# Sketch attention with a gated FFN on one core: S1 and S2 on SyncE's queue, k on ScalarE's, and one weight-narrowing step placed inside the division

## The chip, the cores and the metric

The kernel runs on one core of a Trainium2 chip. The metric is the device time of one execution in microseconds (us), over several runs. A profile of one execution gives the time line: PE is TensorE's matrix multiplication, PEld its weight load, DVE is VectorE, ACT is ScalarE, POOL is GpSimd, SP is SyncE, which here does nothing but issue transfers.

## The reference

There are 4 batches (B) of 4 heads (H), 1088 positions (S) and 32 features (D). Attention uses a polynomial feature map phi with r = 8, so 64 features. Its output, seen as 4352 tokens of 128 features, goes through a gated FFN of width 1536.

```python
def phi(x):
    a = np.einsum('rd,bhsd->bhsr', S1, x)
    b = np.einsum('rd,bhsd->bhsr', S2, x)
    return np.einsum('bhsi,bhsj->bhsij', a, b).reshape(*x.shape[:-1], r * r)
q_p, k_p = (phi(q), phi(k))
kv = np.einsum('bhsf,bhsd->bhfd', k_p, v)
z = np.sum(k_p, axis=2)
num = np.einsum('bhsf,bhfd->bhsd', q_p, kv)
den = np.einsum('bhsf,bhf->bhs', q_p, z)[..., None] + 1e-06
attn = num / den
...
gate = 1.0 / (1.0 + np.exp(-(x @ w_gate)))
out = gate * (x @ w_val) @ w_out
```

S1, S2 and the three weight matrices arrive as 8-byte floating-point numbers, because of a division by a NumPy scalar; q, k and v are 4-byte.

## The kernel before

**The FFN sets the length.** The 4352 tokens are cut into chunks of 512, and the FFN's width into 12 blocks of 128. For one chunk and one block, `w1` multiplies the tokens `xT` with the gate and the value weights into one PSUM tile, `wave` (L314), ACT takes the sigmoid `sg` (L322), `glu` multiplies value and gate to `g` on DVE (L334), and `w2` accumulates g times the output weights in `moeout` (L271). `slot(group, waves)` is the hand-written order: it issues `group` first, then as many rounds of "glu of the wave before, w2 of two waves before, next w1" as `waves` says. All engines but SP run in the order in which the code is written; nothing is reordered.

**Weights are narrowed on the chip.** `load_w(n)` loads two blocks (n from 0 to 5) as pairs of 32-bit words into `w_in`. `narrow` makes 4-byte numbers of them. It is a generator with four steps, so that its instructions can be spread over the code: step 0 is a clamp of the high word on POOL (`cap`, L97) and a scaled copy of the low word on ACT (`tail`, L101). Step 1 is two bit operations on DVE (`head`, L105 and L109), step 2 a square on ACT (L117) and an integer addition on POOL (L118). Step 3 is one DVE instruction that writes `w_sb` (L121). `narrow_w(j, step)` does this for block j from 1 to 11. During the first chunk each `w1` of block j0 issues step 3 of block j0 + 1, step 0 of block j0 + 4, and steps 1 and 2 of block j0 + 2 (L323 to L329). So the wave of block 11 cannot start before step 3 of block 11, which is written down in the `w1` of block 10. S1 and S2 take the same four steps at the very start (`sr_in` to `sr`), with their clamp on DVE.

**Attention of batch 0 comes first,** before any FFN work. S1 and S2 are loaded replicated over the partitions (`load_s`, L129); each is 32 KB in rows of 256 bytes. k of batch 0 is loaded in two parts of 18 and 16 rows per partition, and q in two of 16 and 18 (L224 to L229). The order in the queues is: on SP k's second part, S1, q's first part, v, then weights; on ACT k's first part, S2. DVE then narrows S, transposes k's first part (`turn_k`, L378), makes the sketch matrices `st` and `sk`, transposes k's second part and q's first part (`turn_q`, L389). `kps` on PE (L401) follows, then the outer products `kp`, and `kv0` on PE. Before that PE runs three warm-up multiplications on ones (L243), six instructions in the trace.

**The division.** `dn(b, n)` issues the matmuls for denominators (`dps`, L620) and numerators (`nps`, L631) of one half of batch b: 512 tokens for n = 0, 576 for n = 1. It returns `divide`, which on DVE transposes the denominators, adds, takes the reciprocal (L641 to L644), spreads it with a transpose to `rb` (L648) and multiplies into `xT` (L657). `part(b, n)` issues a pending glu, then dn and its division. For batch 0 the second half is issued at L756 as the group of a slot with two waves; these are the waves of blocks 10 and 11 of the first chunk, and the first chunk needs only tokens of the first half.

Of the kernel before, what the change touches and what calls it, by code (L numbers as in the profile page):

```python
# [20 lines left out]
def kernel(  # L21
# [12 lines left out]
    nc = tc.nc  # L34
# [6 lines left out]
    NJ = DFF // P  # L41
    assert DM == H * D == P and D == 32 and R == 8 and S % 32 == 0

    T = S // 32

    NJK = 9
    KBASE = [0, 9, 17, 25]
# [78 lines left out]

    sr = const.tile([P, 2, D], F32, tag="sr", name="sr")
    sr_in = const.tile([P, 2, D, 2], I32, tag="sr_in", name="sr_in") if wide else None
    def load_s():  # L129
        for n, s_ in enumerate((S1, S2)):  # L130
            rows = bass.AP(tensor=s_.tensor, offset=s_.offset, ap=[[0, P // R], [D, R], [1, D]])
            if wide:
                (nc.sync, nc.scalar)[n].dma_start(
                    out=sr_in[:, n].rearrange("p d w -> p (d w)"), in_=rows.bitcast(I32)
                )
            else:
                (nc.sync, nc.scalar)[n].dma_start(out=sr[:, n], in_=rows)


    w_sb = const.tile([P, 3, NJ, P], F32, tag="w_sb", name="w_sb")  # L140
# [25 lines left out]
    def narrow_w(j, step):  # L166
        if not 0 <= j < NJ:
            return
        n, jj = divmod(j, 2)
        if wide:  # L170
            if step == 0:
                narrowing[j] = narrow(w_sb[:, :, j, :], w_in[n][:, :, jj], nc.gpsimd, j < NJ - 2)
            next(narrowing[j])


    def narrow_0(part, step):
        if wide:
            i = (slice(0, 2), slice(2, 3))[part]
            if step == 0:
                narrowing["0", part] = narrow(w_sb[:, i, 0], w_in[0][:, i, 0], nc.gpsimd)  # L180
            next(narrowing["0", part])


    def load_rows(src, b, t, parts=((0, T, nc.sync),)):
        for t0, t1, eng in parts:
            eng.dma_start(
                out=t[:, t0:t1, :],
                in_=bass.AP(
                    tensor=src.tensor,
                    offset=src[b, 0].offset + t0 * D,  # L190
                    ap=[[T * D, P], [1, (t1 - t0) * D]],
                ),
            )
# [15 lines left out]
    k_t, q_t, v_t = {}, {}, {}  # L209


    def new_kq(b):
        t = ld.tile([P, 2 * H * W1], F32, tag="kq", name="kq")
        kq = t[:, : 2 * T * D].rearrange("p (a t d) -> p a t d", a=2, t=T)
        k_t[b], q_t[b] = kq[:, 0], kq[:, 1]
# [5 lines left out]
            load_rows(q, b, q_t[b])  # L221

    new_kq(0)
    load_rows(k, 0, k_t[0], ((0, KBASE[2] + 1, nc.scalar), (KBASE[2] + 1, T, nc.sync)))  # L224
    load_s()
    load_rows(q, 0, q_t[0], ((0, T0, nc.sync),))
    v_t[0] = load_v(0)
# [74 lines left out]
    def w1():  # L302

        ci = moe["ci"]
        t0, tw = tok_chk[ci]
        jn = TCH // tw
        j0 = moe["w"] * jn
        wv = psm.tile([P, 2, TCH], F32, tag="wave", name="wave")

        tp = tw // 2 if ci == 0 and j0 == 0 else tw  # L310
        for o in range(0, tw, tp):
            for which in range(2):
                for jj in range(jn):
                    nc.tensor.matmul(  # L314
                        out=wv[:, which, jj * tw + o : jj * tw + o + tp],
                        lhsT=w_sb[:, which, j0 + jj, :],
                        rhs=xT[:, t0 + o : t0 + o + tp],
                        start=True,
                        stop=True,
                    )  # L320
        sg = sbG.tile([P, TCH], F32, tag="sg", name="sg", bufs=3)
        nc.scalar.activation(out=sg, in_=wv[:, 0], func=ACTF.Sigmoid)  # L322
        if ci == 0:  # L323
            narrow_w(j0 + 1, 3)
            if j0 == 0:
                narrow_0(1, 3)
            narrow_w(j0 + 4, 0)
            narrow_w(j0 + 2, 1)
            narrow_w(j0 + 2, 2)  # L329


        def glu():
            g = sbG.tile([P, TCH], F32, tag="g", name="g")
            nc.vector.tensor_tensor(out=g, in0=wv[:, 1], in1=sg, op=MUL)  # L334
            moe["todo"].append((ci, j0, jn, g.rearrange("p (j t) -> p j t", j=jn)))

        moe["gate"] = glu
        moe["w"] += 1
        if j0 + jn == NJ:
            moe["ci"] += 1  # L340
            moe["w"] = 0

    def glu():
        if moe["gate"] is not None:
            moe["gate"]()
            moe["gate"] = None

    def slot(group, waves):

        if group is not None:  # L350
            group()
        todo = moe["todo"]
        for _ in range(waves):
            more = moe["ci"] < len(tok_chk)
            if more and sum(tok_chk[moe["ci"]]) > moe["ready"]:
                break
            glu()


            last = moe["ci"] == len(tok_chk) - 1 and moe["w"] > 1  # L360
            lag = 3 if last else 2
            while len(todo) >= lag:
                w2(*todo.pop(0))
            if more:
                w1()
            elif not todo:
                break
            else:
                w2(*todo.pop(0))
# [59 lines left out]
    def half(t, n):  # L429
        return t.rearrange("p (n h w) -> p n h w", n=2, h=H)[:, n, :, : 32 * q_chk[n][1]]  # L430
# [184 lines left out]
    def dn(b, n):  # L615
        t0, tn = q_chk[n]
        w = 32 * tn
        dps = pso.tile([P, TCH], F32, tag=f"acc{(moe['sum'] + 1) % 2}", name="dps")
        for h in range(H):
            nc.tensor.matmul(  # L620
                out=dps[32 * h : 32 * h + 32, :w],
                lhsT=zb[b % 2][:, h, :],
                rhs=half(QP[b], n)[:, 2 * (h % 2) + h // 2, :],
                start=True,
                stop=True,
            )
        t = ps2.tile([P, 2, 512], F32, tag="two", name="nps")
        for h in range(H):
            for c in range(2):
                rows = slice(64 * c, 64 * c + 64)  # L630
                nc.tensor.matmul(  # L631
                    out=t[32 * h : 32 * h + 32, c, :w],
                    lhsT=ND[b][rows, 32 * h : 32 * h + 32],
                    rhs=half(QP[b], n)[rows, 2 * (h % 2) + h // 2, :],
                    start=True,
                    stop=True,
                )

        def divide(*parts):
            dT = sbA.tile([P, 9, 32], F32, tag="dT", name="dT")  # L640
            nc.vector.transpose(out=dT[:, :tn].rearrange("p t c -> p (t c)"), in_=dps[:, :w])  # L641
            rc = sbA.tile([P, 9, 2], F32, tag="rc", name="rc")
            nc.vector.tensor_scalar_add(rc[:, :tn], dT[:, :tn, :2], 1e-6)
            nc.vector.reciprocal(out=rc[:, :tn], in_=rc[:, :tn])  # L644
            rb = sbA.tile([P, 9, 2, 32], F32, tag="rb", name="rb")
            for u0, u1 in parts or [(0, tn)]:
                r0 = rc[:, u0:u1]
                nc.vector.transpose(  # L648
                    out=rb[:, u0:u1].rearrange("p t c s -> p (t c s)"),
                    in_=bass.AP(  # L650
                        tensor=r0.tensor,
                        offset=r0.offset,
                        ap=[list(r0.ap[0]), [1, 2 * (u1 - u0)], [0, 32]],
                    ),
                )
                o = b * S + 64 * (t0 + u0)
                nc.vector.tensor_tensor(  # L657
                    out=xT[:, o : o + 64 * (u1 - u0)].rearrange("p (t c s) -> p c t s", c=2, s=32),
                    in0=t[:, :, 32 * u0 : 32 * u1].rearrange("p c (t s) -> p c t s", s=32),
                    in1=rb[:, u0:u1].rearrange("p t c s -> p c t s"),  # L660
                    op=MUL,
                )
            moe["ready"] = b * S + 64 * (t0 + tn)

        return divide

    steps = narrow(sr, sr_in, nc.vector) if wide else iter(())
    for _ in range(3):
# [5 lines left out]
        out=st_.rearrange("p n u r -> p (n u r)"), in_=sr.rearrange("p n d -> p (n d)")  # L674
# [3 lines left out]
        out=sk,  # L678
# [11 lines left out]
    for n, inner in enumerate(([[1, R], [0, R]], [[0, R], [1, R]])):  # L690
# [3 lines left out]
            out=t, in_=bass.AP(tensor=s0.tensor, offset=s0.offset, ap=[list(s0.ap[0])] + inner)  # L694
# [23 lines left out]
    divide = dn(0, 0)  # L718
# [19 lines left out]
    def q01():  # L738
        spread(0, (1,), qcomp(0, (1,), (ps2, "two")), nc.scalar, nc.sync)

    def part(b, n):
        glu()
        dn(b, n)()

    def kv_all(b):
        kv(b, ZS[b])
# [6 lines left out]
    qmult(0, 1)  # L753
    load_kq(1)
    slot(None, 1)
    slot(lambda: part(0, 1), 2)  # L756
    v_t[1] = load_v(1)
    for b in range(1, B):
        more = b + 1 < B
# [53 lines left out]
```

## Time and profile before

| what | before |
|---|---|
| median of 5 runs | 309.8 us (309.6 to 312.51) |
| the profiled execution | 309.72 us, span 307.9 us |
| PE busy | 299.6 us, 97% of the span |
| DVE busy | 155.6 us, 51% |
| ACT busy | 80.3 us, 26% |
| POOL busy | 34.4 us, 11% |
| granted TensorE clock, mean | 0.999 |
| moved by DMA | 23.37 MB, mean 76 GB/s |

The chain of work that ended last puts 82% of the span on PE, 6% on DMA, 5% on DVE and 3% on POOL. The share of PE is an average: in the first 20 us the matmuls are small and PE waits often, and later it is closed up. The span has 7.7 us in each of the page's 40 slices; the work of the change lies in the first seven of them.

### The profile page before, as it was taken

To read this page: it belongs to the slowest core of one execution; us is meant where nothing else is said; L and a number is where in the kernel's file an instruction comes from. 1 tells how busy PE (TensorE), PEld (TensorE's weight loads), DVE (VectorE), ACT (ScalarE), POOL (GpSimd) and SP (SyncE) were. 2 spreads that over 40 slices of the span, in tenths; PEclk is the share of its full clock that TensorE was granted. 3 is DMA by queue.
4 is the path that set the end of the run, shared out by engine and by line. 5 is a ranking of instruction groups with operands and counts; after the bars stand their busy time and mean duration, and the time that the engine had idled before them with its cause. 6 is when DMAs were issued, how large, how long until landed. Compare 5 with 4: busy or idle time off the path is not lost.

```text
span 307.9 us, 3677 instructions
## 1 busy us (share of the span) xinstructions
PE 299.6 (97%) x1398; PEld 137.1 (45%) x1398; DVE 155.6 (51%) x266; ACT 80.3 (26%) x148; POOL 34.4 (11%) x60
## 2 busy tenths in 40 slices
PE   8889999999999999999999999999999999999994
PEld 2533433444344444443444444344444444444683
DVE  3988789765646554453555542655232223222331
ACT  3345542222122222222123222212222222222220
POOL 1255551320000410000003200000000000000000
PEclk9999999999999999999999999999999999999999
DMA  7992412498402394232004960100001000100021
GB/s 199 354 340 51 148 31 119 88 206 166 146 0 34 94 180 73 56 89 115 2 0 101 177 103 0 32 5 0 0 8 26 2 0 3 31 0 0 6 32 17
DMA packets 29842, 23.37 MB, mean 76 GB/s; under 512 B 21184, under 2 KB 24768, under 8 KB 29824
## 3 DMA queue, kind: packets, MB, share of 16 engines
q1 hardware_dynamic: 25456, 15.51, 18.4%
q0 software_dynamic: 3456, 7.09, 12.9%
q10 hardware_dynamic: 912, 0.54, 0.6%
q8 instruction: 11, 0.18, 0.2%
q14 instruction: 7, 0.06, 0.1%
HBM read 19.86 MB, written 3.26 MB: 75 GB/s over the span
## 4 chain that ended last, share of the span: by engine, by line
PE 82%; DMA 6%; DVE 5%; POOL 3%; issue 1%; ACT 1%; SPq 0%; POOLq 0%; DVEq 0%
PE wave L314 51%; PE moeout L271 26%; POOL head L118 3%; DMA w_in<-in_moe_w_val_dram 3%; DMA w_in<-in_moe_w_out_dram 2%; DVE w_sb L121 2%; DVE head L109 1%; PE kvz L544 1%; DMA kq<-in_k_dram 1%; PE nps L631 1%; PE dps L620 1%; DVE head L105 1%; PE kps L401 1%; PE cqps L487 0%; ACT square L117 0%
## 5 line engine op out<-in xcount | busy, mean ns | idle before, releaser
L314 PE MATMUL wave<-xT,w_sb 128*128 128x512 f32 (+1 forms) x436 | 191.9, 566 | 1.0 <-DVE w_sb L121 0.7
L334 DVE TENSOR_TENSOR g<-wave,sg 128x512 f32<-128x512 f32 x102 | 70.4, 690 | 131.4 <-ACT sg L322 131.1
L314 PEld LDWEIGHTS wave<-xT,w_sb 128*128 128x128 f32 x436 | 82.5, 190 | 95.5 <-issue 87.5
L322 ACT ACTIVATE sg<-wave 128x512 f32<-128x512 f32 x102 | 60.9, 597 | 201.9 <-PE wave L314 199.9
L271 PE MATMUL moeout<-g,w_sb 128*128 128x512 f32 (+1 forms) x216 | 105.4, 576 | 0.2 <-DVE g L334 0.2
L271 PEld LDWEIGHTS moeout<-g,w_sb 128*128 128x128 f32 x216 | 39.5, 190 | 43.8 <-issue 38.7
L511 POOL DMA_DIRECT2D qp<-dq x12 | 7.0, 585 | 110.0 <-DMA dq<-cq 110.0
L118 POOL TENSOR_TENSOR head<-head,tail 128x384 int32<-128x384 int32 (+3 forms) x14 | 13.5, 963 | 21.4 <-DVE head L109 16.5
L420 DVE TENSOR_TENSOR kp<-kab 128x1152 f32<-128x1152 f32 (+3 forms) x12 | 11.4, 986 | 0.0
L520 DVE TENSOR_TENSOR qp<-qp,bq 128x1152 f32<-128x1152 f32 (+1 forms) x7 | 9.1, 1293 | 0.3 <-DMA bq<-dq 0.3
L243 PE MATMUL warm<-ones 128*128 128x512 f32 (+1 forms) x10 | 7.2, 858 | 1.0 <-DVE hm L249 1.0
L281 DVE STREAM_TRANSPOSE o_sb<-moeout 128x512 f32<-128x512 f32 (+1 forms) x9 | 6.1, 679 | 2.6 <-PE moeout L271 2.5
L109 DVE SCALAR_TENSOR_TENSOR head<-cap,head 128x384 int32<-128x384 int32 (+3 forms) x14 | 7.1, 506 | 0.5
L97 POOL TENSOR_SCALAR cap<-w_in 128x384 f32<-128x384 f32 (+2 forms) x13 | 6.7, 520 | 3.7 <-DMA w_in<-in_moe_w_val_dram 3.5
L121 DVE SCALAR_TENSOR_TENSOR w_sb<-square,head 128x384 f32<-128x384 f32 x9 | 5.0, 556 | 4.1 <-POOL head L118 4.1
L511 POOL DMA_DIRECT2D bq<-dq x12 | 6.9, 576 | 0.3
L631 PE MATMUL nps<-qp,nd 64*32 64x256 f32 (+1 forms) x128 | 6.1, 401 | 0.7 <-issue 0.7
L101 ACT ACTIVATE tail<-w_in 128x384 int32<-128x384 uint32 (+2 forms) x13 | 6.6, 521 | 0.0
L657 DVE TENSOR_TENSOR xT<-nps,rb 128x576 f32<-128x576 f32 (+2 forms) x9 | 6.0, 662 | 0.9
L648 DVE STREAM_TRANSPOSE rb<-rc 128x576 f32<-128x576 f32 (+2 forms) x9 | 6.1, 681 | 0.3
L389 DVE STREAM_TRANSPOSE qT<-kq 128x512 f32<-128x512 f32 (+1 forms) x8 | 5.7, 715 | 0.0
L620 PE MATMUL dps<-qp,zb 128*32 128x256 f32 (+1 forms) x64 | 5.3, 404 | 0.1
(59 smaller groups left out, 88.7 us busy)
## 6 DMA issues: line engine op xcount, KB each, us to landing
qp<-dq POOLq DMA_DIRECT2D x12, 288.0 KB, 8.8
bq<-dq POOLq DMA_DIRECT2D x12, 288.0 KB, 9.2
v<-in_v_dram SPq DMA_DIRECT2D x16, 144.0 KB, 5.3
kq<-in_k_dram SPq DMA_DIRECT2D x3, 544.0 KB, 4.0
kq<-in_q_dram SPq DMA_DIRECT2D x3, 544.0 KB, 4.8
w_in<-in_moe_w_gate_dram SPq DMA_DIRECT2D x6, 256.0 KB, 5.4
w_in<-in_moe_w_val_dram SPq DMA_DIRECT2D x6, 256.0 KB, 5.9
w_in<-in_moe_w_out_dram SPq DMA_DIRECT2D x6, 256.0 KB, 6.4
```

What stands on the lines that cost most here:

```text
L109: nc.vector.scalar_tensor_tensor(out=head, in0=cap, scalar=-0x40000000, in1=head, op0=ALU.bitwise_and, op1=ALU.bitwise_or)
L118: nc.gpsimd.tensor_tensor(out=head, in0=head, in1=tail, op=ALU.add)
L121: nc.vector.scalar_tensor_tensor(out=out, in0=square, scalar=1.265625 * 2.0**-30, in1=head.bitcast(F32), op0=ALU.is_ge, op1=MUL,)
L271: nc.tensor.matmul(out=moe["acc"][:, :tw], lhsT=w_sb[:, 2, j, :], rhs=g[:, jj, :tw], start=(j == 0), stop=(j == NJ - 1),)
L314: nc.tensor.matmul(out=wv[:, which, jj * tw + o : jj * tw + o + tp], lhsT=w_sb[:, which, j0 + jj, :], rhs=xT[:, t0 + o : t0 + o + tp], sta ...
L322: nc.scalar.activation(out=sg, in_=wv[:, 0], func=ACTF.Sigmoid)
L334: nc.vector.tensor_tensor(out=g, in0=wv[:, 1], in1=sg, op=MUL)
L420: nc.vector.tensor_tensor(out=KP[b][:, pi, j0:j1].rearrange("p j m (i l) -> p (j m) i l", i=R), in0=bass.AP(tensor=a0.tensor, offset=a0.of ...
L511: get.dma_start(out=t[64 * c : 64 * c + 64, n * H * W1 : (n + 1) * H * W1], in_=bass.AP(tensor=d0.tensor, offset=d0.offset, ap=rows + [[1, ...
L520: nc.vector.tensor_tensor(out=q0, in0=q0, in1=half(BQ[b], n), op=MUL)
L620: nc.tensor.matmul(out=dps[32 * h : 32 * h + 32, :w], lhsT=zb[b % 2][:, h, :], rhs=half(QP[b], n)[:, 2 * (h % 2) + h // 2, :], start=True, ...
L631: nc.tensor.matmul(out=t[32 * h : 32 * h + 32, c, :w], lhsT=ND[b][rows, 32 * h : 32 * h + 32], rhs=half(QP[b], n)[rows, 2 * (h % 2) + h // ...
```

## The change

It does two things. First, S1 and S2 are both issued from SP's queue, ahead of q, and both parts of batch 0's k from ACT's queue. Second, `divide` gets an argument `between`, a function that is called after the transpose to `rb` and before the multiplication into `xT`. For the second half of batch 0 this function is step 3 of block 11's narrowing, which is taken out of the `w1` of block 10. No instruction is added or removed on any engine. On DVE the one L121 instruction and the one L657 instruction change places; on SP the second part of k goes and S2 comes, and on ACT the reverse.

```diff
             if wide:
-                (nc.sync, nc.scalar)[n].dma_start(
+                nc.sync.dma_start(
                     out=sr_in[:, n].rearrange("p d w -> p (d w)"), in_=rows.bitcast(I32)
                 )
             else:
-                (nc.sync, nc.scalar)[n].dma_start(out=sr[:, n], in_=rows)
+                nc.sync.dma_start(out=sr[:, n], in_=rows)
...
-    load_rows(k, 0, k_t[0], ((0, KBASE[2] + 1, nc.scalar), (KBASE[2] + 1, T, nc.sync)))
+    load_rows(k, 0, k_t[0], ((0, KBASE[2] + 1, nc.scalar), (KBASE[2] + 1, T, nc.scalar)))
...
         if ci == 0:
-            narrow_w(j0 + 1, 3)
+            if j0 + 1 < NJ - 1:
+                narrow_w(j0 + 1, 3)
...
-        def divide(*parts):
+        def divide(*parts, between=None):
...
+                if between is not None:
+                    between()
                 o = b * S + 64 * (t0 + u0)
                 nc.vector.tensor_tensor(
...
-    def part(b, n):
+    def part(b, n, between=None):
         glu()
-        dn(b, n)()
+        dn(b, n)(between=between)
...
-    slot(lambda: part(0, 1), 2)
+    slot(lambda: part(0, 1, lambda: narrow_w(NJ - 1, 3)), 2)
```

## The prediction

> **What bounds the kernel now.** I read the page's engine shares first, then TensorE's waits, then the waits and the timeline of VectorE in the two places that the change touches. TensorE (PE) is busy for 97% of the span, so time can only come from where PE idles or starts late. Before 50 us its waits are a list of short ones; from 50 us on there is a single one:
>
> ```profile
> PE wave L314 <- DVE w_sb L121: 0.7, 1, 0.7
> ```
>
> Everything after it is closed up. The windows view (PE, PEld, DVE, ACT, POOL busy; clock; DMA share; GB/s) has PE busy 253.83 of the 253.85 us from there to the last matmul:
>
> ```profile
> 50.25:304.10 253.85, 253.83 (x1070) 117.62 (x1070) 115.35 (x175) 58.16 (x100) 13.29 (x24) 1.00 0.27 54
> ```
>
> So what moves that 50.25 us start earlier moves the end by as much, as long as nothing new becomes late behind it. The timeline of VectorE (DVE) ahead of it (start, duration) shows why PE waited:
>
> ```profile
> 47.07 0.47 DVE L641 STREAM_TRANSPOSE dT<-dps 128x288 f32<-128x288 f32 x1
> 47.58 0.17 DVE L643 TENSOR_SCALAR rc<-dT 128x18 f32<-128x18 f32 x1
> 47.79 0.27 DVE L644 RECIPROCAL rc<-rc 128x18 f32<-128x18 f32 x1
> 48.09 0.78 DVE L648 STREAM_TRANSPOSE rb<-rc 128x576 f32<-128x576 f32 x1
> 48.97 0.76 DVE L657 TENSOR_TENSOR xT<-nps,rb 128x576 f32<-128x576 f32 x1
> 49.64 0.55 DVE L121 SCALAR_TENSOR_TENSOR w_sb<-cap,head 128x384 f32<-128x384 f32 x1
> 50.11 0.68 DVE L334 TENSOR_TENSOR g<-wave,sg 128x512 f32<-128x512 f32 x1
> ```
>
> Block 11's weights (w_sb) stand last in line behind the whole division, though their inputs had been there since 47.7 (POOL's head at 46.72, 1.00 us). The other place is the start, again DVE:
>
> ```profile
> DVE cap L97 <- DMA sr_in<-in_S_dram: 3.5, 1, 3.5
> ```
>
> ```profile
> 4.86 0.20 DVE L97 TENSOR_SCALAR cap<-sr_in 128x64 f32<-128x64 f32 x1 [3.50 <-DMA sr_in<-in_S_dram]
> ...
> 5.46 0.77 DVE L378 STREAM_TRANSPOSE kT<-kq 128x576 f32<-128x576 f32 x1
> 6.15 0.18 DVE L121 SCALAR_TENSOR_TENSOR sr<-cap,head 128x64 f32<-128x64 f32 x1
> 6.37 0.24 DVE L673 STREAM_TRANSPOSE st<-sr 128x64 f32<-128x64 f32 x1
> 6.65 0.19 DVE L677 TENSOR_TENSOR sk<-st,hm 128x32 f32<-128x32 f32 x1
> 6.76 0.70 DVE L378 STREAM_TRANSPOSE kT<-kq 128x512 f32<-128x512 f32 x1
> 7.38 0.67 DVE L389 STREAM_TRANSPOSE qT<-kq 128x512 f32<-128x512 f32 x1
> ```
>
> DVE can do nothing for 3.50 us until S1 and S2 have landed, and from there to 19 us it is busy 0.78 to 1.00 of every microsecond. From 9 to 50 us it waits only 4.6 us in all, each time for POOL inside the narrowing loop. The chain that ended last names weight transfers before 21 us, but these rows say that in the first 20 us the DVE queue is the line in which work stands.
>
> **The narrowing step.** Nothing is added; one DVE instruction changes place with one other. Starts on DVE are spaced 0.88 (rb to xT, which waits for rb), 0.67 (xT to w_sb) and 0.47 (w_sb to g). The step does not depend on rb, so it can start some 0.67 after rb's 48.09, at 48.78, end at 49.33 and let PE start 0.06 later as now, at 49.39. PE itself is free at 49.36: its last pair of moeout matmuls starts at 48.50, and in the closed-up stretch two take 0.86. So PE starts 50.25 - 49.39 = 0.86 us earlier at best; the idle of 0.72 that the timeline states (its matmul ends are modelled) is the lower end. I take 0.8. What pays: xT starts at 49.25 instead of 48.97 and ends at 50.0. Its readers are the waves of tokens 512 to 1023, at 52.93 now and 52.1 then, and batch 1's kps, which reuses the nps buffer at 54.74: 2 us of cover; without it each 0.1 us of late xT would be 0.1 us of PE. g of block 10 follows at 49.9 (now 50.11), before its reader at 51.2. The kT and qT transposes behind it keep their places; k of batch 1 was issued at 44.26 and takes 4.0 us, so it is there at 48.3, 2 us before its transpose.
>
> **The loads.** No DMA and no byte is added. SP issues S1, S2, q's first part, v; ACT issues both parts of k. Issue times in the trace: 0.68 and 0.65 for S, 0.39 and 0.42 for k. SP's q and v go out 0.65 - 0.39 = 0.26 later, ACT's table load starts 0.26 earlier, and the only reader of what that load serves comes at 20.66. The semaphores on which SP waits further down belong to the same four transfers, each landed by 4.86, so the weight issues (4.85 on) stay.
>
> When does each operand land? Windows over the first microseconds give the bytes moved: 442 KB by 3.3 us, 566 by 3.7, 885 by 5.0, 986 by 5.3. The parts are k 295 and 262 KB, S 2 x 33, q 262. k complete fits 3.7 us, and SP's first wait for k's first part ended at 4.47, so 0.77 us lie between last byte and signal. Now S stands behind k in both queues; then S2 is issued at 1.4, its bytes start to move 0.9 later (0.74 to 1.6 for the first transfer now), and it should land near 3.6, 1.2 us earlier. k's first part: 295 + 65 + some 80 KB of q = 440 KB, 3.3 us, landing 4.1. k's second part is the one that pays. Here two rules of the Trainium skill speak against the change ("DMA: Bandwidth & Descriptors"). "Issuing engines are not separate DMA queues" says that all queues run on the same 16 engines and that spreading starts saves only issue time. By that alone a move of 32 KB would be worth the 0.26 us of issue, or nothing. "Queues, rings and completion order" says that a ring is served in order and the engines alternate between the rings. The trace agrees that k's two parts, one per queue, landed close together (4.47, and at most 4.85), so I take even shares, and order within a ring then matters: k's second part has its 262 KB and as many of SP's still ahead, 440 + 524 = 964 KB, 5.25 us, landing 6.0. Its transpose starts at 6.76 now. So the head of the kernel gains 0.76 by that operand, against 1.2 by S alone and 0.26 by the first rule. PE's warm-up matmuls are a second lid: six at a pitch of 0.857 from 0.96 hold PE until 6.1, against 6.89 for kps now, which is 0.8 again. I take 0.8, with ends at 0 and 1.2.
>
> This shift is carried along if later transfers keep up. v is read at 10.30, then 9.5; with 1492 KB moved by 7.5 us (v complete at 1474) it lands at 8.3. Block 2's weights are read by ACT at 15.79, then 15.0; 3328 KB are moved by 12.9, so they land near 13.7. That 1.3 us is the least cover; a shift beyond it would be lost. Between 26.3 and 44.5 PE is closed up (18.20 of 18.20 us), but it only follows its own start at 18.63, so it moves as a whole. The product with bq at 42.89 waits for a DMA that starts from cq at 27.28 and moves with it.
>
> **Sum.** 0.8 + 0.8 = 1.6 us. The profiled execution took 309.72 us (span 307.9, the rest around it), 0.08 below the median of 309.8: 309.72 - 1.6 = 308.1, and about 308.2 by the median. I say 308.1. A comparison of this kernel cannot tell less than about 1% (3.1 us) from no change, so this is "within 1%": faster needs 306.7, slower 312.9.
>
> **Rivals.**
> 1. The head gives nothing (0.10). S comes early but DVE then stands at k's second part, landing at 6.7 or later. For it: that part now stands behind its first part, and bytes before the kernel's first product are unchanged. Against it: the byte count above. Time: 309.72 - 0.8 = 308.9.
> 2. The narrowing step gives nothing (0.06): PE at 49.4 is held by something that the present wait hides, such as g or a wave buffer. Against it: that buffer is free when g of block 9 ends, 47.15. Time: 308.9.
> 3. Slower (0.05): ACT's ring gets no even share, and k's second part is served after all that SP has put in by 4.8 us, S, q and v. That makes 1474 KB, 7.5 us, landing 8.2; its transpose, and with it the whole DVE line, starts 1.45 later than now. Less 0.8 from the narrowing step this is 0.65 slower: 310.4. It decides from a landing at 7.6 on. Against it: the two parts of k side by side in the trace of before.
> 4. The rest (0.04) lies beyond both, as with a PE that restarts at the warm-up's pitch of 0.857 instead of 0.43 us per matmul.
>
> **How the numbers follow.** The forecast has 0.75; its own ends are 0.4 + 0.7 = 1.1 and 1.2 + 0.86 = 2.1 us, so 307.6 to 308.6. Rivals 1 and 2 reach 309.0; with a little for the spread of a median the range is 307.4 to 309.3. Both signs of more than 1% need a cause that I do not see: 0.03 faster, 0.04 slower, 0.93 within.
>
> **What would show it.** In the profile after: cap of sr_in starts near 3.6 instead of 4.86; the second kT transpose near 6.0 with a short DVE wait for k ahead of it; kps at 6.1; the first wave at 17.8 instead of 18.63; w_sb of block 11 ahead of xT; PE's wait of 0.7 for w_sb gone or below 0.1. I am wrong if the second kT starts at 6.7 or later, if the first wave moves by less than half of what kT did, or if PE shows a new wait after its 50 us mark.

## The result, and the profile after

The changed kernel takes 309.05 us (median of 28 runs), the kernel before 310.02 us (49 runs). The ratio is 0.9971, with a 95% interval of 0.9958 to 0.9984: about 0.9 us less, within 1%. (Each ratio here is taken over the undisturbed runs and not from the two medians, so it can differ a little from their quotient.) The profiled execution took 309.11 us with a span of 307.3 us, against 309.72 and 307.9 before.

The end of the division, from VectorE's (DVE's) timeline of the changed kernel (start, duration, engine, line, operation, out<-in):

```profile
48.33 0.78 DVE L650 STREAM_TRANSPOSE rb<-rc 128x576 f32<-128x576 f32 x1
49.04 0.52 DVE L121 SCALAR_TENSOR_TENSOR w_sb<-cap,head 128x384 f32<-128x384 f32 x1
49.47 0.74 DVE L661 TENSOR_TENSOR xT<-nps,rb 128x576 f32<-128x576 f32 x1
50.14 0.68 DVE L336 TENSOR_TENSOR g<-wave,sg 128x512 f32<-128x512 f32 x1
50.74 1.30 DVE L380 STREAM_TRANSPOSE kT<-kq 128x1088 f32<-128x1088 f32 x1
```

and TensorE (PE) beside it:

```profile
48.77 1.02 PE L272 MATMUL moeout<-g,w_sb 128*128 128x512 f32 x2
49.63 1.53 PE L315 MATMUL wave<-xT,w_sb 128*128 128x512 f32 x3
```

w_sb now precedes xT. Block 11's wave starts 0.86 us after the moeout pair, which is the pitch of a closed-up pair, and no wait stands on its row. The only wait of 0.1 us or more that PE had after 50 us is gone, and none has come in its place.

The head of the kernel, DVE's timeline again:

```profile
5.13 0.19 DVE L97 TENSOR_SCALAR cap<-sr_in 128x64 f32<-128x64 f32 x1 [3.78 <-DMA sr_in<-in_S_dram]
...
5.73 0.77 DVE L380 STREAM_TRANSPOSE kT<-kq 128x576 f32<-128x576 f32 x1
6.42 0.18 DVE L121 SCALAR_TENSOR_TENSOR sr<-cap,head 128x64 f32<-128x64 f32 x1
6.64 0.25 DVE L677 STREAM_TRANSPOSE st<-sr 128x64 f32<-128x64 f32 x1
6.92 0.19 DVE L681 TENSOR_TENSOR sk<-st,hm 128x32 f32<-128x32 f32 x1
7.03 0.70 DVE L380 STREAM_TRANSPOSE kT<-kq 128x512 f32<-128x512 f32 x1
```

Here nothing was gained. DVE still waits for S, now for 3.78 us, and everything behind it is 0.27 later than before. The first wave starts at 18.91 instead of 18.63, block 11's wave at 49.63 instead of 50.25. From one to the other it is 30.72 us instead of 31.62. So this pair of profiles shows 0.90 us won in the loop and 0.28 lost in the head. Whether the 0.28 belongs to the change had to be tested.

When S really came through shows in the DMA view by windows of 0.2 us. The packets under 512 bytes are the rows of S, 128 for each of S1 and S2, and some 16 more for every transfer: with S first they come to 288, twice 144, by 3.1 us, and to 576 by 3.5 us in the experiment below that loads each S twice. Of the sums of 304 to 320, 48 to 64 are thus not rows. This count is my table of those windows, with two experiments told of below ("S first": both S ahead of k, one on each queue; "k2 behind S": k's second part behind S1 and S2 on SP):

| window, us | before | after | k2 behind S | S first |
|---|---|---|---|---|
| 2.1 to 2.5 | 0 | 0 | 0 | 16 |
| 2.5 to 2.7 | 0 | 0 | 0 | 93 |
| 2.7 to 2.9 | 0 | 15 | 32 | 169 |
| 2.9 to 3.1 | 0 | 56 | 59 | 10 |
| 3.1 to 3.3 | 1 | 72 | 94 | 0 |
| 3.3 to 3.5 | 19 | 13 | 56 | 0 |
| 3.5 to 3.7 | 84 | 25 | 4 | 2 |
| 3.7 to 3.9 | 99 | 21 | 29 | 5 |
| 3.9 to 4.1 | 80 | 83 | 6 | 7 |
| 4.1 to 4.3 | 32 | 30 | 25 | 1 |
| 4.3 to 4.5 | 5 | 3 | 6 | 1 |

After the change S1 comes 0.6 us earlier, done by about 3.3. But cap waits for both, and S2's rows still pass between 3.5 and 4.4, where the last S passed in the kernel before. S2 had been issued by SP at 1.49 (SP's timeline of the changed kernel):

```profile
1.49 0.57 SPq L134 DMA_DIRECT2D sr_in<-in_S_dram  x1
```

One window of the changed kernel, 2.7 to 3.0 us (q1 is SP's queue, q10 ACT's; packets, MB, share of the 16 engines):

```profile
DMA packets 85, 0.11 MB, mean 364 GB/s; under 512 B 41, under 2 KB 41, under 8 KB 85
...
q10 hardware_dynamic: 50, 0.10, 88.1%
q1 hardware_dynamic: 35, 0.01, 12.8%
```

ACT's queue, with k, has 88% of the engines' time, SP's with S1 13%. In packets it is 50 to 35: the shares are far from even in bytes, and nearer to it in packets, since a row of S has 256 bytes where one of k has 2 KB and more.

### The profile page after: what moved, and what is told of

Same layout as the page of the kernel before. It is cut to its first block, busy times and chain, and to the rows that moved or that the text cites. A ratio compares the mean times of both kernels' runs of the same rounds, so it can differ in the third digit from the quotient of the medians.

```text
span 307.3 us, 3677 instructions
## 1 busy us (share of the span) xinstructions
PE 299.3 (97%) x1398; PEld 137.1 (45%) x1398; DVE 155.3 (51%) x266; ACT 80.3 (26%) x148; POOL 34.6 (11%) x60
## 4 chain that ended last, share of the span: by engine, by line
PE 92%; DVE 5%; DMA 1%; issue 1%; SPq 0%; POOL 0%; POOLq 0%; DVEq 0%
PE wave L315 56%; PE moeout L272 29%; PE nps L633 1%; PE dps L622 1%; PE kvz L546 1%; DMA sr_in<-in_S_dram 1%; PE kps L403 1%; DVE kp L422 1%; PE cqps L489 1%; DVE head L105 1%; DVE head L109 1%; DVE qp L469 0%; DVE w_sb L121 0%; DVE xT L661 0%; DVE kab L413 0%
## 5 line engine op out<-in xcount | busy, mean ns | idle before, releaser
L121 DVE SCALAR_TENSOR_TENSOR w_sb<-square,head 128x384 f32<-128x384 f32 x9 | 5.0, 556 | 4.1 <-POOL head L118 4.1
```

## The experiments

After the result I held these readings against each other. *Start order*: transfers of the two queues begin one after another, so a small one lands by its place in the joint order, and one of the two S is the last of the four in both orders of loads; the loads are then worth nothing, and the narrowing step is all of the gain. *Bytes*: a transfer lands when the bytes ahead of it have moved, as I had counted. Under both, k's second part could be the next thing that DVE stands at.

All diffs are against the changed kernel unless said otherwise. Ratios are to the kernel before on the same chip in the same session.

**The narrowing step alone.** The loads of before are put back.

```diff
-                nc.sync.dma_start(
+                (nc.sync, nc.scalar)[n].dma_start(
...
-    load_rows(k, 0, k_t[0], (..., (KBASE[2] + 1, T, nc.scalar)))
+    load_rows(k, 0, k_t[0], (..., (KBASE[2] + 1, T, nc.sync)))
```

> The narrowing step inside the division alone, loads as before. If the loads of the change cost 0.28 us (first wave at 18.91 instead of 18.63) and the step gains 0.9, this is 0.9 us faster than before (ratio 0.9971): cap of sr_in at 4.86, first wave at 18.63, wave of block 11 at 49.35. If instead the loads are neutral on average and the profile of the change caught a late landing, it is as fast as the whole change (ratio 0.997) and a sum of both parts cannot be told apart here.

308.97 us, ratio 0.9969 (0.9958 to 0.998). Its first wave starts at 18.50, block 11's at 49.25: 30.75 us between them, as in the changed kernel. So this one step gives as much as the whole change. The same loads as before gave cap at 5.09 here, against 4.86 there, so 0.23 us lie between two profiles of one order of loads.

**The loads alone.** The kernel before, with only its loads changed.

> The loads of the change alone, narrowing as before. Theory of turns (SP and ACT start their transfers one at a time, and S2 is the fourth in both orders): cap of sr_in at 4.9 to 5.2, time 0 to 0.3 us above before (ratio 1.000 to 1.001). Theory of bytes (S lands late because of the bytes that the 16 engines carry before it, and the profile of the change caught a bad case): cap near 4.2, time 0.5 us or more below before (ratio 0.998).

309.89 us, ratio 0.9994 (0.9985 to 1.0002): no difference. In the profile, which is of the fastest of its executions (309.23 us), cap starts at 4.69, and the wait that the narrowing step removes is still there (PE's timeline):

```profile
49.74 1.13 PE L314 MATMUL wave<-xT,w_sb 128*128 128x512 f32 x2 [0.73 <-DVE w_sb L121]
```

The first wave is at 18.09, so 31.65 us lie before the wave of block 11. The changed order of loads gave cap at 5.13, 4.69, and 4.95 to 5.14 in three experiments below; the order of before gave 4.86 and 5.09, and 6.44 once, further down. The two orders overlap, and the 0.28 lost in the head of the first profile is no effect of the change.

**S first on both queues.** S1 on SP, S2 on ACT, then k's first part on ACT and its second on SP.

```diff
-    load_rows(k, 0, k_t[0], ((0, KBASE[2] + 1, nc.scalar), (KBASE[2] + 1, T, nc.scalar)))
     load_s()
+    load_rows(k, 0, k_t[0], ((0, KBASE[2] + 1, nc.scalar), (KBASE[2] + 1, T, nc.sync)))
```

> The change with S1 first on SP, S2 first on ACT, then k's first part on ACT and its second on SP. Theory of turns: S1 and S2 are the first and second to start (1.6 and 2.3 us), land near 3.5, cap of sr_in at 3.6; k's first part starts third, lands near 4.7 and its transpose becomes what DVE waits for, at 4.7 instead of 5.46; first wave at 17.9, total 1.6 us below before (ratio 0.995). Theory of bytes: S has few bytes ahead of it here too, so also early; what tells the theories apart is the next kernel. If S takes its 3.5 us from issue to landing whatever stands before it, cap stays at 4.3 or later and the time at that of the narrowing step alone.

309.14 us (307.5 to 316.24), ratio 0.9978 (0.9962 to 0.9995). S does land early here, but DVE soon meets the next wait (its timeline):

```profile
3.35 0.20 DVE L97 TENSOR_SCALAR cap<-sr_in 128x64 f32<-128x64 f32 x1 [2.00 <-DMA sr_in<-in_S_dram]
...
6.08 0.78 DVE L380 STREAM_TRANSPOSE kT<-kq 128x576 f32<-128x576 f32 x1 [2.04 <-DMA kq<-in_k_dram]
```

The wait for k ends 0.95 us later than the one for S did after the change. S2 was issued at 0.75, k's first part behind it at 1.47, and k's bytes on ACT's queue began only near 3.7, after SP's k had been moving since 2.9. The window of 3.0 to 3.6 us:

```profile
DMA packets 67, 0.14 MB, mean 229 GB/s; under 512 B 0, under 2 KB 0, under 8 KB 67
...
q1 hardware_dynamic: 67, 0.14, 71.5%
```

There is no row for ACT's queue, though it has had work since 1.5 us and the engines have room. A count of bytes cannot explain that; a joint order of starts would, though this does not show it.

**The same with k's first part on SP.** SP's part of k had begun first there, so k's first part is put on SP and the second on ACT.

```diff
-    load_rows(k, 0, k_t[0], ((0, KBASE[2] + 1, nc.scalar), (KBASE[2] + 1, T, nc.scalar)))
     load_s()
+    load_rows(k, 0, k_t[0], ((0, KBASE[2] + 1, nc.sync), (KBASE[2] + 1, T, nc.scalar)))
```

(S1 on SP, S2 on ACT as before.)

> The change with S1 and k's first part on SP, S2 and k's second part on ACT, S first on both. With S first on both and k's parts the other way round, S landed for 3.35, the part on SP started at 2.85, and the part on ACT at 3.65, landing at 6.08. If that was the order in which the two queues are served, k's first part now lands at 4.3 to 4.8, its transpose starts there instead of at 5.7, and the second transpose at 6.1 is the next wait: kab at 7.6 to 7.8, first wave at 17.5 to 18.1, ratio to before 0.994 to 0.995. If ACT's part goes first this time, the first transpose waits until 5.5 or later and the time is as with the change.

307.98 us, ratio 0.9928 (0.9908 to 0.9949). DVE's timeline:

```profile
3.21 0.20 DVE L97 TENSOR_SCALAR cap<-sr_in 128x64 f32<-128x64 f32 x1 [1.85 <-DMA sr_in<-in_S_dram]
...
5.26 0.78 DVE L380 STREAM_TRANSPOSE kT<-kq 128x576 f32<-128x576 f32 x1 [1.37 <-DMA kq<-in_k_dram]
```

S early again, and k's first part still waits behind it, for 1.37 us. This time ACT's part began first, near 2.7, and SP's near 3.4, so again the first part was the later one; it was complete 0.8 us sooner than in the run above. In these two runs, then, the issuing engine does not settle which queue goes first. Block 11's wave, at 48.56, is 1.07 us ahead of the changed kernel's: 0.47 by kab (8.08 for 8.55), the rest by shorter products on DVE (2.86 us for 3.45, see the last section), and that these are due to the loads is not shown.

**k's second part behind S on SP.** ACT loads only k's first part.

```diff
-    load_rows(k, 0, k_t[0], ((0, KBASE[2] + 1, nc.scalar), (KBASE[2] + 1, T, nc.scalar)))
+    load_rows(k, 0, k_t[0], ((0, KBASE[2] + 1, nc.scalar),))
     load_s()
+    load_rows(k, 0, k_t[0], ((KBASE[2] + 1, T, nc.sync),))
```

> The change with k's second part on SP behind S1 and S2, so that only k's first part runs on ACT beside S. Theory of sharing (S1 and S2 are stretched by k's packets on the same engines: 0.8 us each in the change against some 0.4 with few bytes beside them): S1 and S2 end at 3.1 and 3.5 us, cap of sr_in at 4.0 to 4.2, k's second part lands near 5.2, first wave 17.6 to 18.0, total 0.8 us below the change (ratio to before 0.994 to 0.995). Theory of a late start (S2's first packet comes 2.1 us after its issue whatever runs beside it): cap at 4.7 or later, total as the change (0.997).

308.69 us, ratio 0.995 (0.9931 to 0.997), whose interval overlaps that of the change. cap starts at 4.72. S2 is now third, and its rows begin right behind S1's near 3.2; yet the last of them pass only by 4.4. The engines are far from full meanwhile (window of 3.6 to 3.9 us):

```profile
DMA packets 42, 0.03 MB, mean 90 GB/s; under 512 B 33, under 2 KB 33, under 8 KB 42
...
q1 hardware_dynamic: 42, 0.03, 38.7%
```

So a place earlier in the order brings S2's start forward, but not its end by as much. The start order fits when the transfer begins; what slows S2's rows here stays open. The count of bytes misses as well: few bytes move.

**Two small transfers ahead of k.** S1 and S2 are loaded once more into a tile `spare` that nothing reads, on ACT ahead of k.

```diff
+    if wide:
+        spare = const.tile([P, 2, D, 2], I32, tag="spare", name="spare")
+        for n, s_ in enumerate((S1, S2)):
+            rows = bass.AP(tensor=s_.tensor, offset=s_.offset, ap=[[0, P // R], [D, R], [1, D]])
+            nc.scalar.dma_start(
+                out=spare[:, n].rearrange("p d w -> p (d w)"), in_=rows.bitcast(I32)
+            )
```

> The change with two more transfers of S1 and S2 into an unused tile, issued on ACT ahead of k; S1 and S2 proper stay first on SP. So S2 proper is the fourth to start, but only 98 KB stand ahead of it instead of some 400. Theory of turns: cap of sr_in stays at 4.6 to 5.2. Theory of bytes: S2 lands by 3.7, cap near 3.8. k lands later than before by either, so the first wave is late by either.

One run, 310.75 us. cap started at 3.86, near the 3.8 that bytes had named, and not at the 4.6 or later that a fixed cost for each turn had given. So a place in the order has no fixed cost here. By the first packets in windows of 0.1 us, a transfer begins 0.4 to 1.3 us behind a part of k and 0.2 to 0.5 behind an S (kernels before and after, both runs with S first, and k's second part behind S). The price was k: its first transpose waited until 6.28 (1.74 us). The granted clock then fell to 0.50 to 0.65 from 9 to 13 us, and the first wave came at 20.95.

**S on POOL's queue.** S1 and S2 are issued by POOL, k by ACT and SP as before.

```diff
-                nc.sync.dma_start(
+                nc.gpsimd.dma_start(
```

> The change with S1 and S2 on POOL's queue, ahead of POOL's other work, and k's two parts on ACT and SP as before the change. If S is held up by standing behind k in the two hardware queues, it now starts beside k and lands at 3.5 to 4.2; k's parts land at 4.5 at most; first wave 17.7 to 18.1, ratio to before 0.994 to 0.995. If the engines shared with k are what stretches S, it still lands at 4.7 or later, ratio 0.997.

312.65 us, ratio 1.0072 (1.0046 to 1.0098): slower, by 0.7%. POOL issued at 1.26; that queue's first packets came near 4.0, and cap started at 7.40. The first wave came at 22.83, 3.92 us later than after the change, though cap was only 2.27 later: the granted clock was 0.72 from 9 to 12 us, 0.50 from 12 to 15 and 0.64 from 15 to 18. All 11 executions had a mean clock below 0.995 (0.983 to 0.994).

**S without company.** k's loads were written behind ACT's table load, to give S the queues to itself.

> The change with ACT's table load ahead of k's two transfers, so that k is issued at 2.1 instead of 0.74 and S1 and S2 start with nothing beside them. If k's company is what holds S (its engines or its place in line), S lands by 3.9, cap of sr_in at 3.9 or earlier. If two small transfers one behind the other on one queue take that long by themselves, cap stays at 4.5 or later. k lands 1.3 later in either case, at 5.1 or later, so its first transpose becomes DVE's wait.

One run, 309.48 us; the edit did not do what it was meant to. ACT's timeline:

```profile
0.74 1.28 ACT L246 ACT_TABLE_LOAD   x1 [0.74 <-PEq L801]
0.94 0.89 ACTq L187 DMA_DIRECT2D kq<-in_k_dram  x2
```

The issue of k came 0.2 us after the table load began and did not wait for it. S had company as ever, and cap started at 5.45.

**The narrowing step still earlier,** before the rb transpose instead of behind it.

```diff
+                if between is not None:
+                    between()
                 nc.vector.transpose( ... rb ... )
-                if between is not None:
-                    between()
```

> The change with block 11's last narrowing step one place further ahead, before the transpose to rb. If PE's own end of the pair of moeout matmuls is what now holds the wave of block 11, nothing more is gained: that wave starts 30.6 to 30.8 after the first wave (30.72 in the change, 31.62 before it), and xT's end moves by nothing. If the narrowing step still holds it, the wave comes up to 0.6 earlier, 30.1 after the first.

DVE finished w_sb at 48.64, 0.9 us before PE took it, and PE gained nothing: 30.73 us from the first wave (18.82) to block 11's (49.55). PE's own moeout pair is now what ends there. The one run took 310.26 us; what it has more than the changed kernel lies later. PE's waits after 50 us:

```profile
PE moeout L272 <- DVE g L336: 1.0, 1, 1.0
```

DVE was held there by batch 1's `bq` arriving late from DMA. A twin of this wait, 1.4 us, shows in one of two profiles of the next kernel, so it comes and goes with the execution.

**k transposed before S is narrowed.** The loads now bring k's first part early, at a time when DVE waits for S. So DVE takes k's first transpose ahead of S's clamp, and its second ahead of the rest of S's chain.

```diff
+    turn_k(0, 0, KBASE[2] + 1)
...
-    turn_k(0, 0, KBASE[2] + 1)
+    turn_k(0, KBASE[2] + 1, T)
...
-    turn_k(0, KBASE[2] + 1, T)
```

> The change with DVE's order at the start altered: k's first transpose ahead of S's narrowing, the second one in the gap before its last step. No transfer is moved. In the change k's first part landed 3.1 us after its issue, so at 3.85, and DVE stood idle until 5.13. Both transposes then cost DVE nothing: cap of sr_in unchanged (4.7 to 5.1), sk at cap + 1.8, but kab at sk + 0.9 instead of sk + 1.6, so the first wave 0.6 to 0.7 earlier relative to cap (13.1 instead of 13.8, or 12.7 instead of 13.4), total 0.6 us below the change (ratio to before 0.995). If k's second part lands after 5.6, the gain is less.

308.35 us, ratio 0.992 (0.9885 to 0.9955). The profiled execution was 310.84 us, long for this kernel: besides the late bq its clock was near half from 9 to 12.6 us. The same kernel once more:

> The kernel with k's transposes early and the loads of the change once more, beside the same with the old loads. Its first profile had TensorE at a granted clock of 0.50 from 9.0 to 12.5 us and showed the gain only up to kab (sk + 1.07 instead of sk + 1.63). Without that stretch the first wave should come 13.1 or 12.7 after cap (by whether the kp products take 3.45 or 3.09), with a median 0.5 to 0.7 below the change, ratio to before 0.9945 to 0.9955.

307.73 us (4 runs, 307.56 to 307.94), ratio 0.9908 (0.9893 to 0.9924), the lowest of all, though its interval overlaps that of S first with k's first part on SP. DVE's timeline:

```profile
3.68 0.78 DVE L380 STREAM_TRANSPOSE kT<-kq 128x576 f32<-128x576 f32 x1 [2.32 <-DMA kq<-in_k_dram]
4.95 0.20 DVE L97 TENSOR_SCALAR cap<-sr_in 128x64 f32<-128x64 f32 x1 [0.50 <-DMA sr_in<-in_S_dram]
...
5.55 0.70 DVE L380 STREAM_TRANSPOSE kT<-kq 128x512 f32<-128x512 f32 x1
...
6.68 0.19 DVE L682 TENSOR_TENSOR sk<-st,hm 128x32 f32<-128x32 f32 x1
...
7.75 0.85 DVE L413 STREAM_TRANSPOSE kab<-kps 128x288 f32<-128x288 f32 x2 [0.16 <-PE kps L403]
```

Two transposes of k fit into the wait for S, and the kab transpose moves from 8.55 after the change to 7.75. The first wave starts at 17.75, block 11's at 48.49: 1.14 us ahead of the changed kernel. Of that, 0.18 is S (cap at 4.95 for 5.13), some 0.6 the new order, and 0.36 shorter products on DVE (3.09 us for 3.45). Neither k transpose waits late: the first part is there at 3.68, the second by 5.55. The gain forecast for this order was 0.5 to 0.7 us, which the 0.6 bears out; but the ratio is 0.0063 below that of the change, nearly 2 us. The two ratios come from different chips, and what the profile does not account for stays unexplained.

**The same with the loads of before.**

> DVE's altered order (k's transposes around S's narrowing) with the loads of before. In four profiles the loads of the change made S land no earlier, but k's first part 0.5 to 0.8 earlier (3.7 to 3.85 against 4.47 and 4.6). If that is what they are worth, k's first transpose now starts at 4.5 and ends at 5.3, cap of sr_in waits for DVE at 5.2 instead of 4.7 to 5.1 for S, and this is 0.2 to 0.4 us slower than the next kernel. If the loads are worth nothing with this order either, the two are within 0.15 us.

310.91 us (308.41 to 312.33), ratio 0.9992 (0.9969 to 1.0016): the gain is gone. The first part of k is there at 4.64 instead of 3.68. S came at 6.44 in this profile, later than in any other with these loads, and PE then waited 3.0 us for sk. The windows view (length, busy time and number of instructions of PE, PEld, DVE, ACT, POOL; granted clock; DMA share; GB/s) has

```profile
6.00:7.00 1.00, 0.00 (x0) 0.00 (x0) 0.49 (x3) 0.26 (x1) 0.00 (x0) 1.00 1.07 180
7.00:8.00 1.00, 0.00 (x0) 0.00 (x0) 0.96 (x4) 0.26 (x1) 0.32 (x1) 0.82 1.08 208
8.00:9.00 1.00, 0.58 (x16) 0.23 (x16) 0.95 (x3) 0.39 (x2) 0.21 (x1) 0.50 1.10 170
```

PE is idle from 6 to 8 us and starts again at half clock, which lasts until after 14 us; the first wave is at 20.95. By their ratios the two orders of loads differ here by about 2.6 us. Much of that goes with the clock: 12 of the 14 executions had a mean granted clock below 0.995, and the two others took 308.41 and 308.79 us, 0.7 and 1.1 above the same order with the new loads. How much of this is k's earlier landing and how much a late S, one profile cannot say.

## Why the prediction was wrong about the loads and right about the narrowing step

The forecast was 1.6 us, two terms of 0.8. About 0.9 came: one term held, and the other was worth nothing.

**The narrowing step: right.** The prediction had 0.8 us, between 0.72 and 0.86; the profiles show 0.90 from first wave to block-11 wave, a little more than its upper end, and the step alone, by its ratio of 0.9969, is 0.0031 x 310.02 = 0.96 us. PE's lid was as said: the wave starts at the end of the moeout pair, and nothing earlier on DVE helps. The late xT, the late g and the kT behind them cost nothing, as forecast; PE has no new wait.

**The loads: wrong, by all of their 0.8 us.** The step that failed is "S2 is issued at 1.4, its bytes start to move 0.9 later". S2 was issued at 1.49 and its rows began near 3.6, 2.1 us later, and were through by 4.4, as before. S was ready at 5.13 instead of 3.6, and 1.2 of these 1.5 us are that start. The 0.9 was read from the first transfer of the kernel, when nothing else was under way, and applied to the fourth. (In windows of 0.1 us that first transfer moves nothing before 1.7, so even its delay was 1.0.) The trace of before already held the better number: there both S were issued at 1.19, and the first rows came between 3.4 and 3.5 for S2 on ACT's queue and at 3.6 for S1 on SP's, 2.2 to 2.4 us later. So S1 was the last one before and S2 is after, and not S2 in both, as the expectation of the loads alone has it: the change swapped which S comes late. I had only used that trace's sums of bytes, which do not tell whose they are. Why a transfer in that place starts so late is not shown; the order of starts is the reading that fits most of the runs. With S not early, the estimate of 6.0 for k's second part carried no weight: that part was there by 5.55 in the run that asks for it first, earlier than reckoned, but DVE in the changed order comes to it only at 7.03, behind S.

**The even shares: wrong in bytes.** Between 2.7 and 3.0 us the queues had 88% and 13% of the engines; SP's packets are small there. Taking even shares was a step of the prediction's own, and it made k's second part late: all 288 packets of ACT's queue, both parts of k, had passed by 4.2 us, where the prediction had the last byte at 5.25 and the landing at 6.0. Of the two rules weighed, the Trainium skill's "Issuing engines are not separate DMA queues" ("DMA: Bandwidth & Descriptors"), by which spreading starts saves only issue time, would have given 0 to 0.26 us and was the nearer; the loads alone measured a ratio of 0.9994.

**The rivals.** Rival 1 named the outcome, 308.9, with the head giving nothing; but not the cause. It had DVE standing at k's second part, and DVE stood at S, as before. Rivals 2 and 3 did not come. The range held the measured time only because it reached to rival 1, which had been given 0.10; that the time fits it is luck, since its cause did not come. Of the signs to look for, two came true (w_sb ahead of xT, PE's wait gone) and those of the head failed: cap at 5.13 for 3.6, the second kT at 7.03 for 6.0, the first wave at 18.91 for 17.8.

**What the loads do give.** The first part of k lands earlier, because the second part no longer moves beside it on SP's queue. From 2.5 to 2.7 us the kernel before has

```profile
q1 hardware_dynamic: 17, 0.03, 48.7%
q10 hardware_dynamic: 16, 0.04, 46.5%
```

and the changed kernel, with k's first part alone,

```profile
q10 hardware_dynamic: 34, 0.08, 99.3%
```

In the changed kernel DVE has been told to do S first and cannot use it. With the order turned round it does: 307.73 us.

**What stays open.** What makes a load begin so late behind others; why S2's rows pass so slowly in the run with k's second part behind S; and why the same loads land S 0.2 to 0.5 us apart from one execution to the next, and once 1.5. Each S load reads the same 2 KB sixteen times over, for the 128 partitions; that was the same in all runs, so no run tells whether it matters.

## What to carry to other kernels

Take the delay of a load from a transfer that stands at the same place among its neighbours, not from the first one of the kernel; and ask which of several awaited loads lands last, since moving the other is worth nothing. On an engine that runs in written order, let the work whose operands come first stand first: here that gave the lowest ratio, but only together with the loads that bring those operands early. Where an in-order engine has a step without near dependencies, put it ahead of the long chain that it would otherwise wait behind, up to the point where the consumer's own queue is the bound.

## What the runs showed of the hardware

**The products on DVE were longer by about 0.6 us with a POOL clamp inside them.** The six kp products of batch 0 took about 2.86, 3.09 or 3.45 us together. They took 3.42 to 3.47 in the nine profiles where POOL's clamp of 128x384 lay wholly inside them, 3.08 or 3.09 in the three where it reached over their end, and 2.86 in the two where it lay before or behind them. The timeline of DVE and POOL in the kernel before:

```profile
9.04 3.45 DVE L420 TENSOR_TENSOR kp<-kab 128x512 f32<-128x512 f32 x6
...
11.28 0.60 POOL L97 TENSOR_SCALAR cap<-w_in 128x384 f32<-128x384 f32 x1 [0.21 <-DMA w_in<-in_moe_w_out_dram]
```

3.45 - 2.86 = 0.59, beside that clamp's 0.60. But the agreement is of this profile alone: in the nine profiles the clamp took 0.54 to 0.84 us, and the products grew by 0.56 to 0.61 whatever its length. The time goes on to the first wave: it starts 13.77 us behind cap in before, 13.78 after, and 13.41 and 13.40 with the narrowing step alone and the loads alone, where the clamp reaches over the end. I read this over the profiles and did not test it by an edit.

**The clock can fall in the head of the kernel.** In four of the 14 profiles it was 1.00 for PE's warm-up and near 0.50 some microseconds later. Three of these had a late S or k and PE idle behind its warm-up: two small transfers ahead of k, S on POOL's queue, and k transposed early with the old loads; their first waves came at 20.95 to 22.83. But the first profile of k transposed early (the first list) had S at 5.14, no later than the changed kernel, and the second profile of the same kernel (the second list) kept 1.00. The windows of both, with the columns as above:

```profile
8.00:9.00 1.00, 0.56 (x17) 0.14 (x15) 1.00 (x3) 0.46 (x1) 0.00 (x0) 1.00 0.97 231
9.00:10.00 1.00, 1.00 (x19) 0.85 (x22) 1.00 (x3) 0.13 (x1) 0.00 (x0) 0.52 1.03 369
10.00:11.00 1.00, 1.00 (x20) 0.24 (x15) 1.00 (x3) 0.59 (x1) 0.49 (x1) 0.50 1.08 377
```

```profile
8.00:9.00 1.00, 0.66 (x18) 0.26 (x14) 1.00 (x3) 0.55 (x1) 0.00 (x0) 1.00 1.04 300
9.00:10.00 1.00, 1.00 (x36) 0.53 (x26) 1.00 (x3) 0.54 (x2) 0.00 (x0) 1.00 1.07 371
10.00:11.00 1.00, 1.00 (x67) 0.82 (x57) 1.00 (x4) 0.08 (x1) 0.21 (x1) 1.00 1.06 377
```

The busy time of PE differs by a tenth of a microsecond in the slice before the fall. PE had waited 1.0 us for sk in the first and 0.5 in the second; but with the narrowing step alone, the loads alone and S without company it waited 1.3 to 1.7 us at that place and kept 1.00. What decides it is not shown. What the runs show is what can go with a late operand there: with S on POOL's queue, 2.27 us of it became 3.92 at the first wave.
